# Score blocks of the agent-attention and squared-ReLU kernel: their TensorE passes get the scheduler's highest priority

## The chip, the cores and the metric

The kernel runs on one core of one Trainium2 chip. The metric is the device time of one execution in microseconds (us). All times of the profile's rows count from the start of its span.

## The reference

Per batch (4 batches, 12480 tokens of 128 channels, 49 agents), attention goes through the agents, and its output goes through a two-layer network with a squared ReLU:

```python
a2k = sm(agents, k)            # softmax over the 12480 keys, scale 1/sqrt(128)
agent_v = a2k @ v
q2a = sm(q, agents)            # softmax over the 49 agents
x = (q2a @ agent_v).reshape(49920, 128)
h = np.maximum(x @ w_in, 0.0)  # 2048 columns
out = h * h @ w_out
```

All data are float32.

## The kernel before

**The main chain.** The attention's last product and the first layer are folded: a table per batch (`aw_hi` and `aw_ex`, 98 agent rows in high and low parts by 2048 columns) lets the first layer read the query weights (`w` and `x`) directly. A query block has 960 tokens, in two halves of 480 (the constant `G`). For each half the loop over `k` goes through 2048 columns in 8 steps of two groups of 128 columns. The loop issues two steps at a time, which is called a *round* here: 416 rounds in all, 8 to a query block. In a round TensorE does 12 passes of the second layer for earlier steps (`second`, tile `o`, three passes for each of four column groups: high by high, high by low, low by high), then 4 passes `h<-w,aw_hi` and 4 short passes `h<-x,aw_ex` (`first`, two tiles `h` of two banks each, from a pool of three). ScalarE (ACT) then does for each `h` tile a ReLU (`r`) and a square (`g_hi`), VectorE (DVE) the product `r*h` (into `gg`, or back into `h`), and DVE or GpSimd (POOL) the low part `g_lo`. `queued` ties each of these instructions behind the one before it on its engine, so that the main chain's own order on each engine is fixed; all of them are recorded at line 59, because `queued` issues them.

**The work beside it.** Queries of later blocks (`queries`) and keys and values of the next batch (`background`) are generators. `step` takes a few of their steps per round; from then on a scheduler decides, by priority and by a simulated time line, where their instructions stand among those of the main chain, since they are only tied behind the prologue. By default priority follows the order in which the code was recorded. All that work shares one PSUM bank, the pool `ps_a` with the tile `psa`, in turns: score blocks of keys (`psa<-ag,kt`) or queries (`psa<-ag,qt`), transposes of the query weights (`psa<-identr,pp`, line 381, two groups of 4 per query block), value sums (`psa<-vs,e`, 8 passes, line 302) and table pieces.

**A score block.** `scores` and `queries` call `tiled` for each of 8 groups of 120 or 128 tokens, and `tiled` cuts a group into strips of 32 tokens (`CT`): each strip is loaded as the stationary operand and writes 32 partitions of `psa`. A block is 32 such passes of 49 columns; in the trace each float32 pass is two matmuls, so a block shows as x64. After the block DVE takes the maximum (`m`, line 362) and the difference (`e`, line 364) of a query block, ACT the exponential, DVE the sum and its inverse (`z`, lines 369 to 371), POOL the product and the low part of the weights, and PE the transposes, from which ACT copies `w` (line 386). Small DMAs on SyncE's queue then fill the rest of `w` and `x`. `w` and `x` have two buffers per half, so that a block's weights lie where those of the block two before lay.

The main chain's own short passes already stand in such a context (`first`):

```python
with tc.high_priority():
    for t, out in enumerate(outs):
        rows = slice(t * 32, t * 32 + NL)
        queued(nc.tensor.matmul, nc.tensor, out, state[b]["lo"][rows, c // 2, :], x[rows, :], start=False, stop=True)
```

Of the kernel before, what the change touches and what calls it, by code (L numbers as in the profile page):

```python
# [32 lines left out]
CT = 32  # L33
# [4 lines left out]
def agent_attention_relu2(ctx: ExitStack, tc: tile.TileContext, qT, kT, v, agT, w_in, w_out, outT):  # L38
# [36 lines left out]
    pe, act, dve, pool, sync = (Ordered(e) for e in (nc.tensor, nc.scalar, nc.vector, nc.gpsimd, nc.sync))  # L75
# [22 lines left out]
    for base in (NA, -NA):  # L98
        nc.gpsimd.affine_select(
            out=quad.rearrange("p h a -> p (h a)"), in_=quad.rearrange("p h a -> p (h a)"),  # L100
# [76 lines left out]

    def tiled(out, stationary, moving):
        n = stationary.shape[1]
        for at in range(0, n, CT):  # L180
            up = min(at + CT, n)
            pe.matmul(out[at:up, :], stationary[:, at:up], moving, start=True, stop=True)  # L182

    def scores(b, i, kt):
        st = state.setdefault(b, {"s": []})
        _, rows, nt = blocks[i]
        if alone[0]:
            h = ps_h.tile([P, 2, 512], F32, name="h")[:rows, :, :].rearrange("p h (t x) -> p h t x", x=P)
            n = nt // 2
            for t in range(nt):  # L190
                out = h[:, t // n, t % n, : 2 * NA]
                keys = kt[:, t * rows : (t + 1) * rows]
                pe.matmul(out, keys, ag[:, :2, :].rearrange("c b a -> c (b a)"), start=True, stop=True)
            sv = h[:, :, :n, :NA]
        else:
            sv = bank()[:rows, : nt * NA].rearrange("p (t a) -> p t a", a=NA)
            for t in range(nt):
                tiled(sv[:, t, :], kt[:, t * rows : (t + 1) * rows], ag[:, b, :])
        yield
        s = sp.tile([P, NT, NA], F32, name="s")  # L200
        st["s"].append(s)
        if i == 0:
            st["mx"] = small.tile([P, NT, NA], F32, name="mx")
        s, mx = (x[:rows, :nt, :] for x in (s, st["mx"]))
        if alone[0]:
            s, mx = (x.rearrange("p (h t) a -> p h t a", h=2) for x in (s, mx))
        if i == 0:
            dve.tensor_copy(mx, sv)
        else:
            dve.tensor_max(mx, mx, sv)  # L210
        act.copy(s, sv)  # L211
# [139 lines left out]
    def queries(g):  # L351
# [6 lines left out]
        for t in range(NT):  # L358
            tiled(sv[:, t, :], qt[:, t * TP : (t + 1) * TP], ag[:, b, :])
# [140 lines left out]
    with tc.tile_pool(name="pre", bufs=PRE) as pre, tc.tile_pool(name="dec", bufs=2) as dec:  # L500
# [39 lines left out]
        for i in range(NK):  # L540
# [9 lines left out]
            if i in between:  # L550
                n = between[i]
# [82 lines left out]
```

## Time and profile before

| | |
|---|---|
| median of 3 runs | 2038.29 us (2037.62 to 2038.71) |
| profiled execution | 2038.58 us, its span 2036.8 us, so 1.78 us lie around the span |
| granted TensorE clock over the span | 0.99 |
| TensorE (PE) busy | 1993.6 us, 98% of the span |
| ACT, DVE, POOL busy | 1776.5, 1663.8, 1271.1 us |

The first 105 us or so are a prologue (weights, keys and values of the first batch); the rest is the 416 rounds. PE, the matmul row, counts as busy from the start of a matmul to its modelled end, and neighbours overlap; how much time a piece of work takes from the others is therefore read from starts: how long after the first `o` pass of one round the first `o` pass of the next one begins.

### The profile page before, as it was taken

To read this page: it belongs to the slowest core of one execution; us is meant where nothing else is said; L and a number is where in the kernel's file an instruction comes from. 1 tells how busy PE (TensorE), PEld (TensorE's weight loads), DVE (VectorE), ACT (ScalarE), POOL (GpSimd) and SP (SyncE) were. 2 spreads that over 40 slices of the span, in tenths; PEclk is the share of its full clock that TensorE was granted. 3 is DMA by queue.
4 is the path that set the end of the run, shared out by engine and by line. 5 is a ranking of instruction groups with operands and counts; after the bars stand their busy time and mean duration, and the time that the engine had idled before them with its cause. 6 is when DMAs were issued, how large, how long until landed. Compare 5 with 4: busy or idle time off the path is not lost.

```text
span 2036.8 us, 40065 instructions
## 1 busy us (share of the span) xinstructions
PE 1993.6 (98%) x15188; PEld 1493.9 (73%) x15188; DVE 1663.8 (82%) x1843; ACT 1776.5 (87%) x2100; POOL 1271.1 (62%) x1103
## 2 busy tenths in 40 slices
PE   8599999999999999999999999999999999999999
PEld 8477777777777777777777777777777777777777
DVE  5678888888888888888888888888888888888887
ACT  2388999989888999999898899998998989889897
POOL 2555877766555687776565577776555656556565
PEclk8799999999999999999999999999999999999999
DMA  8243121121123221211113212211111111111100
GB/s 311 86 139 92 62 63 51 63 73 50 48 69 97 71 66 59 72 46 63 58 36 97 88 43 68 63 58 41 38 46 45 34 44 34 41 43 38 41 25 27
DMA packets 55976, 131.89 MB, mean 65 GB/s; under 512 B 6712, under 2 KB 35336, under 8 KB 55784
## 3 DMA queue, kind: packets, MB, share of 16 engines
q1 hardware_dynamic: 55784, 129.33, 19.8%
q8 instruction: 120, 1.97, 0.4%
q14 instruction: 72, 0.59, 0.1%
HBM read 80.97 MB, written 25.56 MB: 52 GB/s over the span
## 4 chain that ended last, share of the span: by engine, by line
PE 50%; DMA 1%; DVE 1%; ACT 1%; issue 0%; SPq 0%; ACTq 0%; DVEq 0%
PE o L59 31%; PE h L59 16%; PE psa L182 2%; PE psa L381 1%; DMA kt<-in_kT 0%; PE psa L302 0%; PE psa L335 0%; DMA x<-w 0%; ACT r L59 0%; DVE gg L59 0%; DVE h L59 0%; DVE g_lo L59 0%; ACT g_hi L59 0%; DVE ob L59 0%; SPq L391 0%
## 5 line engine op out<-in xcount | busy, mean ns | idle before, releaser
L432 POOL TENSOR_TENSOR g_lo<-gg,g_hi 128x480 fp32r<-128x480 f32 x832 | 999.5, 1223 | 684.1 <-DVE gg L59 534.9
L59 ACT ACTIVATE r<-h 128x960 f32<-128x960 f32 x832 | 801.2, 963 | 127.2 <-PE h L59 120.1
L59 ACT ACTIVATE g_hi<-r 128x960 fp32r<-128x960 f32 x832 | 837.7, 1007 | 32.7 <-issue 0.4
L59 DVE TENSOR_TENSOR h<-r,h 128x960 f32<-128x960 f32 x416 | 481.9, 1158 | 166.3 <-ACT r L59 165.8
L59 DVE TENSOR_TENSOR gg<-r,h 128x960 f32<-128x960 f32 x416 | 477.5, 1148 | 82.6 <-ACT r L59 76.1
L59 PE MATMUL o<-g_hi,wo_hi 128*128 128x480 f32 x1664 | 538.3, 404 | 0.0
L59 DVE TENSOR_TENSOR g_lo<-h,g_hi 128x960 fp32r<-128x960 f32 x416 | 480.4, 1155 | 36.6 <-ACT g_hi L59 7.9
L59 PE MATMUL h<-w,aw_hi 128*128 128x480 f32 x1664 | 493.6, 403 | 15.9 <-DVE gg L59 13.5
L59 PE MATMUL o<-g_lo,wo_hi 128*128 128x480 f32 x1664 | 495.0, 378 | 0.0
L59 PE MATMUL o<-g_hi,wo_lo 128*128 128x480 f32 x1664 | 494.5, 378 | 0.0
L59 PEld LDWEIGHTS o<-g_hi,wo_hi 128*128 128x128 f32 x1664 | 280.3, 188 | 118.4 <-issue 78.0
L59 PEld LDWEIGHTS o<-g_hi,wo_lo 128*128 128x128 f32 x1664 | 312.5, 188 | 47.4
L59 PEld LDWEIGHTS o<-g_lo,wo_hi 128*128 128x128 f32 x1664 | 312.8, 188 | 46.9
L59 PEld LDWEIGHTS h<-w,aw_hi 128*128 128x128 f32 x1664 | 283.5, 189 | 76.2 <-DVE gg L59 27.8
L59 PE MATMUL h<-x,aw_ex 19*128 19x480 f32 x1664 | 205.8, 480 | 1.0 <-DMA x<-w 0.9
L59 PEld LDWEIGHTS h<-x,aw_ex 19*128 19x128 f32 x1664 | 80.4, 181 | 142.1 <-issue 138.3
L59 DVE COPY ob<-o 128x480 f32<-128x480 f32 x104 | 68.3, 657 | 42.7 <-PE o L59 42.6
L237 POOL TENSOR_TENSOR vs<-vt,vs 128x1024 fp32r<-128x1024 f32 (+1 forms) x39 | 81.7, 2096 | 5.6 <-ACT vs L235 5.4
L182 PEld LDWEIGHTS psa<-ag,qt 128*32 128x32 f32 (+1 forms) x3200 | 47.4, 107 | 50.7 <-issue 44.8
L182 PE MATMUL psa<-ag,qt 128*32 128x49 f32 (+1 forms) x3200 | 68.2, 211 | 0.0
L381 PEld LDWEIGHTS psa<-identr,pp 120*98 120x98 f32 x408 | 51.1, 166 | 9.0 <-ACT s L211 0.7
L386 ACT CAST w<-psa 98x480 fp32r<-98x480 f32 x102 | 55.6, 545 | 1.7 <-PE psa L381 1.5
(113 smaller groups left out, 965.1 us busy)
## 6 DMA issues: line engine op xcount, KB each, us to landing
qt<-in_qT SPq DMA_DIRECT2D x52, 480.0 KB
out_T<-ob SPq DMA_DIRECT2D x104, 240.0 KB
kt<-in_kT SPq DMA_DIRECT2D x36, 512.0 KB
vt<-in_v SPq DMA_DIRECT2D x36, 512.0 KB
x<-w SPq DMA_DIRECT2D x416, 35.6 KB
ahead<-in_kT SPq DMA_DIRECT2D x12, 512.0 KB
ahead<-in_v SPq DMA_DIRECT2D x12, 512.0 KB
w<-w SPq DMA_DIRECT2D x104, 56.2 KB
```

Source lines behind the costliest of these rows:

```text
L59: ins = issue(*args, **kw)
L182: pe.matmul(out[at:up, :], stationary[:, at:up], moving, start=True, stop=True)
L237: eng.tensor_sub(out[:, :, n : n + w], x, out[:, :, :w].bitcast(F32))
L381: pe.matmul(pt[:K2, t * TP : (t + 1) * TP], pp[:, j * (NT // 2) + t, :], identr, start=True, stop=True)
L386: act.copy(w[:K2, :], pt[:K2, :G])
L432: nc.gpsimd.tensor_sub(lo[:, n, :], gg[:, n, :], hi[:, n, :].bitcast(F32))
```

## The change

`tiled` opens a context of highest priority around its loop, so that the scheduler takes the passes of one call as soon as they are ready, before any other ready instruction of TensorE. No instruction is added or removed, no size, tile or buffer is changed.

```diff
     def tiled(out, stationary, moving):
         n = stationary.shape[1]
-        for at in range(0, n, CT):
-            up = min(at + CT, n)
-            pe.matmul(out[at:up, :], stationary[:, at:up], moving, start=True, stop=True)
+        with tc.high_priority():
+            for at in range(0, n, CT):
+                up = min(at + CT, n)
+                pe.matmul(out[at:up, :], stationary[:, at:up], moving, start=True, stop=True)
```

What the scheduler makes of it can be read from the order in which the built programs issue their instructions. Before, 51 of the 86 blocks of 32 passes beside the main chain stand in one piece and 35 in several: 15 in five pieces (9, 4, 8, 4 and 7 passes), 3 in five (9, 8, 9, 3 and 3), and 17 in three (7, 6, 19 or near it). Together the 35 blocks have 106 pieces more than blocks. Now all 86 are in one piece. The three tail blocks of 6 passes were whole and are.

On PE, at a key block of the third batch that stood in three pieces before (tiles `w` and `x` are the query weights of the block in work):

```order
L59 MATMUL o<-g_lo,wo_hi 128x480 x2
L182 MATMUL psa<-ag,kt 32x49 x9
L59 MATMUL h<-w_6083,aw_hi 128x480 x2
L182 MATMUL psa<-ag,kt 32x49 x4
L59 MATMUL h<-w_6083,aw_hi 128x480 x2
L59 MATMUL h<-x_6084,aw_ex 128x480 x4
```

The third piece, of 19 passes, stands in the round behind. Now, on PE at a key block of the same stretch:

```order
L59 MATMUL o<-g_lo,wo_hi 128x480 x2
L183 MATMUL psa<-ag,kt 32x49 x32
L59 MATMUL h<-w_6032,aw_hi 128x480 x4
L59 MATMUL h<-x_6033,aw_ex 128x480 x4
L59 MATMUL o<-g_hi,wo_hi 128x480 x2
```

The block moved into one place, between the second layer's passes and the first layer's.

On PE, in the last batch, the query block of tile `psa_19791` before (its first two pieces; three more follow in the next two rounds):

```order
L59 MATMUL o_19693<-g_lo_19613,wo_hi_108 128x480 x2
L182 MATMUL psa_19791<-ag_82,qt_19751 32x49 x3
L182 MATMUL psa_19791<-ag_82,qt_19751 24x49
...
L59 MATMUL h_19713<-w1_19239,aw_hi_17165 128x480 x2
L182 MATMUL psa_19791<-ag_82,qt_19751 32x49 x2
...
L59 MATMUL h_19714<-w1_19239,aw_hi_17165 128x480 x2
L59 MATMUL h_19713<-x1_19240,aw_ex_17166 128x480 x2
```

And the same block now:

```order
L59 MATMUL o_19307<-g_lo_19281,wo_hi_108 128x480 x2
L183 MATMUL psa_19791<-ag_82,qt_19751 32x49 x3
L183 MATMUL psa_19791<-ag_82,qt_19751 24x49
...
L59 MATMUL h_19367<-w0_19188,aw_hi_17165 128x480 x2
L59 MATMUL h_19368<-w0_19188,aw_hi_17165 128x480 x2
L59 MATMUL h_19367<-x0_19189,aw_ex_17166 128x480 x2
```

It became whole, and it stands 7 rounds earlier among the passes of the main chain. From the second batch's values on, most of the work on `psa` moved up by 6 to 10 rounds with it, transposes and value sums too.

On ACT, the copy of the transposed query weights into `w0_19960` before (line 386; `r` and `g_hi` are the main chain's):

```order
L59 ACTIVATE r_19994<-h_19964 128x960
L59 ACTIVATE g_hi_19997<-r_19994 128x960
L386 CAST w0_19960<-psa_19955 98x480
L59 ACTIVATE r_20024<-h_20014 128x960
L59 ACTIVATE g_hi_20028<-r_20024 128x960
```

And now:

```order
L59 ACTIVATE r_19516<-h_19485 128x960
L59 ACTIVATE g_hi_19519<-r_19516 128x960
L387 CAST w0_19960<-psa_19955 98x480
L59 ACTIVATE r_19540<-h_19530 128x960
L59 ACTIVATE g_hi_19544<-r_19540 128x960
```

The copy kept its place behind a `g_hi`, but it moved 10 rounds up. There the round's last passes that read `w0_19188`, whose buffer `w0_19960` takes over, stand directly behind the transposes on PE, where before they lay rounds back.

## Rows read from the trace of the kernel before

**Rows 1.** The page: busy time by engine, share of the span, instructions.
```profile
PE 1993.6 (98%) x15188; PEld 1493.9 (73%) x15188; DVE 1663.8 (82%) x1843; ACT 1776.5 (87%) x2100; POOL 1271.1 (62%) x1103
```

**Rows 2.** Busy time by stretch: stretch, its length, then PE, PEld, DVE, ACT, POOL.
```profile
300.00:400.00 100.00, 99.58 (x631) 75.95 (x630) 83.90 (x90) 95.28 (x114) 74.90 (x63) 1.00 0.18 58
...
1503.00:1975.00 472.00, 472.00 (x3042) 344.66 (x3041) 391.38 (x411) 421.44 (x473) 273.53 (x236) 1.00 0.12 39
```

**Rows 3.** Waits, whole program: who waited for whom, us in total, times, longest.
```profile
ACT r L59 <- PE h L59: 120.1, 171, 1.2
...
PE h L59 <- DVE gg L59: 13.5, 15, 7.0
...
PEld h L59 <- DMA x<-w: 3.5, 8, 0.8
```

**Rows 4.** Timeline of PE, a round without other work: start, length, instruction.
```profile
1678.93 0.69 PE L59 MATMUL o<-g_hi,wo_hi 128*128 128x480 f32 x2
...
1683.00 0.70 PE L59 MATMUL o<-g_hi,wo_hi 128*128 128x480 f32 x2
```

**Rows 5.** Timeline of PE, two rounds that each hold a whole block.
```profile
604.73 0.70 PE L59 MATMUL o<-g_hi,wo_hi 128*128 128x480 f32 x2
...
609.85 0.70 PE L59 MATMUL o<-g_hi,wo_hi 128*128 128x480 f32 x2
...
634.99 0.70 PE L59 MATMUL o<-g_hi,wo_hi 128*128 128x480 f32 x2
...
637.77 0.89 PE L182 MATMUL psa<-ag,qt 128*32 128x49 f32 x64
...
640.07 0.70 PE L59 MATMUL o<-g_hi,wo_hi 128*128 128x480 f32 x2
```

**Rows 6.** Timeline of PE, three rounds that hold a block in five pieces.
```profile
1664.26 0.69 PE L59 MATMUL o<-g_hi,wo_hi 128*128 128x480 f32 x2
...
1667.06 0.45 PE L182 MATMUL psa<-ag,qt 128*32 128x49 f32 x18
...
1669.35 0.69 PE L59 MATMUL o<-g_hi,wo_hi 128*128 128x480 f32 x2
...
1677.15 0.37 PE L182 MATMUL psa<-ag,qt 128*32 128x49 f32 x14
```

**Rows 7.** Timeline of PE: first passes around a three-piece and another five-piece block.
```profile
399.23 0.71 PE L59 MATMUL o<-g_hi,wo_hi 128*128 128x480 f32 x2
...
409.14 0.71 PE L59 MATMUL o<-g_hi,wo_hi 128*128 128x480 f32 x2
...
1224.50 0.71 PE L59 MATMUL o<-g_hi,wo_hi 128*128 128x480 f32 x2
...
1239.25 0.70 PE L59 MATMUL o<-g_hi,wo_hi 128*128 128x480 f32 x2
```

**Rows 8.** Timeline of ACT in the second round of rows 6.
```profile
1669.45 0.97 ACT L59 ACTIVATE r<-h 128x960 f32<-128x960 f32 x1 [1.13 <-PE h L59]
```

**Rows 9.** Timeline of POOL, DVE and PE near 305 us, and line 370's group.
```profile
304.02 2.21 POOL L237 TENSOR_TENSOR vs<-vt,vs 128x1024 fp32r<-128x1024 f32 x1 [0.41 <-ACT vs L235]
...
305.00 1.27 DVE L370 TENSOR_SCALAR z<-z 120x8 f32<-120x8 f32 x1
...
307.38 0.70 PE L59 MATMUL h<-w,aw_hi 128*128 128x480 f32 x2 [0.42 <-DVE gg L59]
...
1650.08 0.16 DVE L370 TENSOR_SCALAR z<-z 120x8 f32<-120x8 f32 x1
...
L370 DVE TENSOR_SCALAR z<-z 120x8 f32<-120x8 f32 x51 | 21.7, 426 | 0.2
```

**Rows 10.** Timeline of PE and ACT at a group of transposes and the copy behind it.
```profile
1658.50 0.48 PE L381 MATMUL psa<-identr,pp 120*98 120x120 f32 x4
1658.81 0.65 PE L59 MATMUL h<-w,aw_hi 128*128 128x480 f32 x2
...
1659.31 0.54 ACT L386 CAST w<-psa 98x480 fp32r<-98x480 f32 x1
```

## The prediction

> **What bounds the kernel now.** I read the page's busy times first: PE is busy for 98% of the span, ACT for 87%, DVE for 82% [rows 1]. A busy PE proves little, since its matmuls overlap in the record, so I looked at two stretches. In the last batch, where only queries run beside the main chain, PE never pauses in 472 us, and ACT works for 421.44 of them, 89%; in the values' stretch PE is busy for 99.58 of 100 us and ACT for 95.28 [rows 2]. Then the waits: ACT waited 171 times for PE's `h`, 120.1 us in all, while PE waited only 13.5 us for DVE's `gg`, of which 7.0 us are one wait [rows 3]. So PE sets the pace of the rounds nearly everywhere, and a microsecond that leaves PE's sequence leaves the time, as long as ACT and DVE can follow. The third view is the timeline of PE, where rounds can be compared from first pass to first pass.
>
> **The change part by part.** A round without other work takes 1683.00 − 1678.93 = 4.07 us [rows 4]. A round with a whole block takes 640.07 − 634.99 = 5.08 us, and another 609.85 − 604.73 = 5.12 us [rows 5]; I take their mean, 5.10, so a whole block costs 1.03 us.
>
> A block in five pieces runs through three rounds, from 1664.26 [rows 6] to 1678.93 [rows 4]: 14.67 us, less three plain rounds (12.21), is 2.46 us. The other kind of five pieces takes 1239.25 − 1224.50 = 14.75 us [rows 7], so 2.54 us. A block in three pieces takes two rounds, 409.14 − 399.23 = 9.91 us [rows 7], less 8.14, so 1.77 us. All have the same 32 passes as a whole block. What they have more is the number of times that PE goes from the main chain's passes of 128 columns to strips of 32 columns and back.
>
> In one piece each saves the difference to 1.03 us: 1.43, 1.51 and 0.74 us. The order of the programs gives the counts: 15, 3 and 17. The sum is 15 × 1.43 + 3 × 1.51 + 17 × 0.74 = 21.45 + 4.53 + 12.58 = 38.6 us. As a check, that is 106 pieces fewer at 0.36 us each, and the three kinds alone give 0.36 (1.43 over four pieces), 0.38 (1.51 over four) and 0.37 (0.74 over two), so the price goes with the number of pieces, whatever their lengths. The 51 blocks that were whole, and the three tails, save nothing.
>
> Does PE's gain reach the end? In the last batch's 13 blocks (18.6 us of the sum) yes by these rows: ACT itself stands for 1.13 us waiting for PE in a round with pieces [rows 8], and ACT's 421.44 us in a stretch that shrinks from 472 to about 453 are 93%. For the other 22 blocks (20.0 us) the room is smaller, because of the 95.28 of 100 us; that is the first rival below.
>
> The moves cost nothing that I can find, but each has a bound. A whole block in front of the four `w` passes gives ACT its next `h` later by up to 1.03 us in one round instead of by less in three; the rounds of rows 5 show it at no cost beyond 1.03. The copy of `w` on ACT, 50 times, now waits for the two `w` passes behind the transposes, the last readers of the buffer that it overwrites. In the row the transposes end at 1658.98, the copy starts at 1659.31, and the two passes end at 1659.46 [rows 10], so the copy would be later by some 0.15 us here and by 0.48 us (1659.46 − 1658.98) if ACT were free at once. I take nothing, since ACT has 0.2 to 0.45 us to spare in a round by its busy shares (5 and 11% of 4.07); the bounds are 50 × 0 and 50 × 0.15 = 7.5 us. SyncE's queue issues the small copies into `x` behind it, and behind those the next query load, outputs and the next batch's keys or values; these are asked for later by the same 0.15 to 0.48 us, but all of the query work stands rounds earlier, so the weights have more time to land than before. That removes at most the 3.5 us in which PE waited for `x` [rows 3].
>
> The inverse of the sums (`z`, DVE, line 370) is the one step that shows how a shift may cost. Its work is tiny, 0.16 us, but beside a value conversion of 2.21 us on POOL it took 1.27 us, the product behind it was late, and PE stood 0.42 us; over all 51 it took 426 ns on the mean [rows 9]. It will still come about two rounds behind its score block, and the value sums move up with it, so that I let it cost what it costs now: a change of 0. [...] The sum by rows alone stays at 38.6 us.
>
> The profiled execution took 2038.58 us (span 2036.8 and 1.78 around it), 0.3 us over the median, which is no difference here. 2038.58 − 38.6 = 2000.0 us. I hold what a measurement can tell from no change to be 0.2%, 4 us.
>
> **The rivals.**
> 1. *ACT or DVE sets the pace where values run.* In the stretch of 300 to 400 us the three split blocks would take 2.2 us out of PE's 99.58, and ACT's 95.28 of 97.8 would be 97%: near enough to full that PE may wait for `h` to come free. For it speaks that these PE waits are already in the trace (0.42 us in rows 9); against it, that all of PE's waits for DVE's `gg` are only 13.5 us now [rows 3]. Half to all of the 20.0 us of the 22 blocks would be lost: 2010 to 2020 us.
> 2. *`z` meets POOL each time* (the other side). The shift brings each query's `z` beside a POOL instruction: 1.27 − 0.16 = 1.11 us on DVE per query block, and if PE follows in full, 50 × 1.11 = 55.5 us, so 2000.0 + 55.5 = 2055.5 us. It decides from 38.6 / 50 = 0.77 us per query block on; the PE wait seen, 0.42 us, is below that. Against it: the last batch has no value conversions, and the mean of 426 ns says that some of it is already paid.
> 3. *The waits go as well.* With query work rounds ahead, PE's waits for `gg` other than the longest (13.5 − 7.0 = 6.5 us) and for `x` (3.5 us) vanish too: 2000.0 − 10.0 = 1990 us. For it speaks only the earlier place.
> 4. *Nothing.* If the pieces only filled time in which PE would have waited anyway, whole blocks leave the same time as waits: 2038 us. Against it: whole blocks in rows 5 cost 1.03 us with no wait beside them, and ACT waited for PE in the pieces' rounds.
>
> **How the numbers follow.** The sum: 0.73, with its own range of 1993 to 2008 (10 us less by rival 3's waits in part, 7.5 us more by the copies). Rival 1: 0.15, of which about half lies below 2013. Rival 2: 0.04. Rival 3 in full: 0.05. Rival 4: 0.03. The prediction is 2000 us. A range of 1990 to 2013 holds the sum, rival 3 and half of rival 1, about 0.85. Faster by over 0.2% are the sum and rivals 1 and 3: 0.93; within 0.2% rival 4: 0.03; slower rival 2: 0.04.
>
> **What would show it.** In the timeline of PE of the changed kernel every block of 32 passes stands as x64, and a round that holds one takes about 5.1 us; the last batch's 8 rounds of a query block last 1.4 us less than before. PE is still busy for 98% or more, over a span of about 1998 us; ACT's and DVE's busy times are what they were, within a few microseconds, and their shares rise by 2%. Rival 1 would show in PE waits for DVE's `gg` that grow by 10 us or more in the values' stretches; rival 2 as a mean of line 370 over 1 us; rival 3 as waits below 8 us. The prediction is wrong if a whole block costs more than 1.03 us in its new place, by a wait for the bank `psa` or for `qt` to land, which PE, serving in order, would pass on to all passes behind it.

## The result and the profile after

The changed kernel takes 2008.97 us (median of 4 runs, 2008.32 to 2009.03) against 2038.16 us for the kernel before in the same comparison: a ratio of 0.9856, with a 95% interval of 0.9839 to 0.9873. It is 29.2 us faster. The prediction was 2000.0 us with a range of 1990 to 2013 us: the direction and the cause held, and 9 us of the gain did not come.

The page's busy times after, as in [rows 1]:

```profile
PE 1960.0 (98%) x15188; PEld 1492.7 (74%) x15188; DVE 1690.4 (84%) x1843; ACT 1777.6 (89%) x2100; POOL 1272.3 (63%) x1103
```

ACT and POOL do what they did, within 2 us. PE's busy time fell by 33.6 us. DVE's rose by 26.6 us, although no instruction was added (23.4 of it in the addition of the query sums, below): that is the first sign of what went wrong. The stretches that answer to [rows 2] (stretch, length, then PE, PEld, DVE, ACT, POOL):

```profile
300.00:400.00 100.00, 99.36 (x691) 76.10 (x690) 84.48 (x93) 95.12 (x114) 76.67 (x64) 1.00 0.20 65
1474.00:1940.00 466.00, 461.34 (x3066) 347.79 (x3066) 411.77 (x411) 428.29 (x480) 278.23 (x239) 1.00 0.12 39
```

In the last batch PE, which never paused before, now stands for 4.7 of 466 us. The values' stretch looks as before. The timeline of PE in the last batch shows where (start, length, instruction; the first `o` passes of four rounds, and the block):

```profile
1579.00 0.69 PE L59 MATMUL o<-g_hi,wo_hi 128*128 128x480 f32 x2
...
1581.80 0.90 PE L183 MATMUL psa<-ag,qt 128*32 128x49 f32 x64
...
1584.11 0.70 PE L59 MATMUL o<-g_hi,wo_hi 128*128 128x480 f32 x2
...
1588.19 0.70 PE L59 MATMUL o<-g_hi,wo_hi 128*128 128x480 f32 x2
...
1592.94 0.70 PE L59 MATMUL o<-g_hi,wo_hi 128*128 128x480 f32 x2
```

The whole block's round takes 5.11 us, as in [rows 5], and the next one 4.08 us, as in [rows 4]. The one after that takes 4.75 us and holds no other work: 0.67 us are lost there. The timeline of the same rounds on DVE, POOL and PE says why:

```profile
1586.39 0.55 DVE L370 TENSOR_REDUCE z<-e 120x8 f32<-120x392 f32 x1
...
1586.94 2.40 POOL L433 TENSOR_TENSOR g_lo<-gg,g_hi 128x480 fp32r<-128x480 f32 x2 [2.46 <-DVE z L370]
1586.97 1.21 DVE L371 TENSOR_SCALAR z<-z 120x8 f32<-120x8 f32 x1
...
1588.22 0.20 DVE L372 RECIPROCAL z<-z 120x8 f32<-120x8 f32 x1
1588.34 1.14 DVE L59 TENSOR_TENSOR h<-r,h 128x960 f32<-128x960 f32 x1
...
1590.69 1.15 DVE L59 TENSOR_TENSOR gg<-r,h 128x960 f32<-128x960 f32 x1
...
1591.89 0.48 PE L59 MATMUL h<-w,aw_hi 128*128 128x480 f32 x1 [0.35 <-DVE gg L59]
```

Eight numbers per partition get 1e-9 added, and it takes 1.21 us: it ends as the first half of POOL's `g_lo`, begun 0.03 us earlier, ends (two halves in 2.40 us). Everything behind it on DVE is late, the product `gg` ends at 1591.84, and PE, which needs the `h` tile that `gg` frees, starts its second pair of `w` passes at 1591.89. Over the program (the group of this line, with its mean in ns, and the wait of PE for `gg` in us, times, longest):

```profile
L371 DVE TENSOR_SCALAR z<-z 120x8 f32<-120x8 f32 x51 | 45.1, 884 | 1.0
```
```profile
PE h L59 <- DVE gg L59: 21.7, 30, 7.4
```

The mean was 426 ns before [rows 9] and the wait 13.5 us [rows 3].

### The profile page after: what moved, and what is told of

Its sections match the earlier page's. It is cut to its first block, busy times and chain, and to the rows that moved or that the text cites. A ratio compares the mean times of both kernels' runs of the same rounds, so it can differ in the third digit from the quotient of the medians.

```text
span 2007.2 us, 40193 instructions
## 1 busy us (share of the span) xinstructions
PE 1960.0 (98%) x15188; PEld 1492.7 (74%) x15188; DVE 1690.4 (84%) x1843; ACT 1777.6 (89%) x2100; POOL 1272.3 (63%) x1103
## 5 line engine op out<-in xcount | busy, mean ns | idle before, releaser
L433 POOL TENSOR_TENSOR g_lo<-gg,g_hi 128x480 fp32r<-128x480 f32 x832 | 1000.6, 1224 | 645.7 <-DVE gg L59 437.0
L59 DVE TENSOR_TENSOR g_lo<-h,g_hi 128x960 fp32r<-128x960 f32 x416 | 480.5, 1155 | 37.7 <-ACT g_hi L59 4.3
L59 PE MATMUL h<-w,aw_hi 128*128 128x480 f32 x1664 | 476.4, 397 | 23.6 <-DVE gg L59 21.7
L59 PEld LDWEIGHTS h<-w,aw_hi 128*128 128x128 f32 x1664 | 290.5, 189 | 87.2 <-DVE gg L59 39.1
L238 POOL TENSOR_TENSOR pp<-e,pp 120x392 fp32r<-120x392 f32 x51 | 49.2, 966 | 3.3 <-ACT pp L236 3.3
L183 PEld LDWEIGHTS psa<-ag,qt 128*32 128x32 f32 (+1 forms) x3200 | 37.9, 108 | 16.7 <-issue 10.3
```

The source lines that it names most:

```text
L59: ins = issue(*args, **kw)
L238: eng.tensor_sub(out[:, :, n : n + w], x, out[:, :, :w].bitcast(F32))
L433: nc.gpsimd.tensor_sub(lo[:, n, :], gg[:, n, :], hi[:, n, :].bitcast(F32))
```

## The experiments

Theory A: the missing 9 us are the addition in `z`, held up beside POOL's `g_lo` and passed on to PE. Theory B: a whole block delays `h`, and ACT and DVE fall behind whatever `z` takes. Eight kernels were run, each against the kernel before, whose median was 2037.62 us beside e1 to e4 and 2037.53 us beside e5 to e8. With the 2038.16 us beside the changed kernel, times of different comparisons carry some 0.6 us against each other.

**e1_no_add.** The changed kernel without the addition.

```diff
         dve.reduce_sum(z, e, axis=AX.X)
-        dve.tensor_scalar_add(z, z, 1e-9)
         dve.reciprocal(z, z)
```

> The changed kernel without line 371, the addition of 1e-9 to the query sums (left out; the sums are at least 1, since each block's maximum is subtracted). Theory A (the 9 us that the change fell short are DVE waits at that addition, which POOL's g_lo holds up for 1.2 us in 34 or so of 50 query blocks): the waits of PE for DVE's gg behind a score block vanish, also those that the kernel before already had; 20 us of lateness over the rounds' medians sit there, so 1989 to 1996 us. Theory B (a whole block makes h late, and ACT and DVE fall behind whatever z takes): only 45 us of DVE time off PE's path goes, at most 2 us less: 2007 to 2009 us.

Measured: 1990.89 us, 0.9773 of the kernel before (0.9759 to 0.9788). Theory A; theory B is out, since leaving out a step that takes 0.16 us when free gave 18.1 us. The same place of the last batch, on DVE and POOL:

```profile
1574.14 0.56 DVE L370 TENSOR_REDUCE z<-e 120x8 f32<-120x392 f32 x1
...
1574.73 0.20 DVE L371 RECIPROCAL z<-z 120x8 f32<-120x8 f32 x1
...
1575.52 1.16 DVE L59 TENSOR_TENSOR h<-r,h 128x960 f32<-128x960 f32 x1 [0.58 <-ACT r L59]
...
1574.70 2.41 POOL L432 TENSOR_TENSOR g_lo<-gg,g_hi 128x480 fp32r<-128x480 f32 x2 [2.80 <-DVE z L370]
```

POOL starts `g_lo` as the sum ends, just as in the changed kernel, and the reciprocal runs beside it in 0.20 us, not held. DVE then even waits for ACT. On PE the rounds behind the block:

```profile
1571.87 0.70 PE L59 MATMUL o<-g_hi,wo_hi 128*128 128x480 f32 x2
...
1575.95 0.70 PE L59 MATMUL o<-g_hi,wo_hi 128*128 128x480 f32 x2
...
1580.14 0.69 PE L59 MATMUL o<-g_hi,wo_hi 128*128 128x480 f32 x2
```

4.08 and 4.19 us, where the changed kernel has 4.08 and 4.75: the held addition costs 0.56 us here. In the last batch PE and ACT run the same instructions in the same order in both kernels (2818 and 459 of them from the 313th product `gg` on), so that the addition alone makes this difference; in the batches before it the order differs in places. PE's waits for `gg` are 10.2 us, of which 7.2 us are one wait in the prologue's end:

```profile
PE h L59 <- DVE gg L59: 10.2, 6, 7.2
```

**e2_before_no_add.** The same line taken out of the kernel before; the blocks are in pieces again.

```diff
-        dve.tensor_scalar_add(z, z, 1e-9)
```

> The kernel before without the same addition (left out). Its order has 131 pieces more than blocks where the kernel before has 106. If each piece costs 0.36 us whatever stands beside it, it lies 131 x 0.36 = 47 us above the changed kernel without the addition: under theory A 2036 to 2043 us, about the kernel before. If pieces only fill time in which PE would wait anyway, it lies within 10 us of the changed kernel without the addition.

Measured: 2035.37 us, 0.9989 (0.9979 to 0.9999). It is 44.5 us above e1, for 131 pieces: 0.34 us each, with no addition in either kernel. This is the price of a piece without the addition, and it agrees with the 0.36 us from rounds of one kernel, although e1 and e2 also differ in where the blocks stand. Pieces do not fill time in which PE would wait here. (The expected 2036 to 2043 was 0.6 us too high at its lower end.)

**e3_two_adds.** The suspected step doubled.

```diff
         dve.tensor_scalar_add(z, z, 1e-9)
+        dve.tensor_scalar_add(z, z, 0.0)
```

> The changed kernel with a second addition (of zero) behind line 371 in each query block. Theory A: the second one meets the second half of POOL's g_lo as the first met the first, 1.2 us more on DVE in some 34 blocks, of which PE pays at least half: 2025 to 2050 us. Theory B: 50 x 0.07 us of DVE time beside the path: 2009 to 2012 us.

Measured: 2055.96 us, 1.0096 (1.0075 to 1.0116): slower than the kernel before, 47.0 us above the changed kernel, and 6 us more than theory A's upper end. Both additions are held; in the last batch the first ends with the first half of `g_lo` and the second with the second (1.22 us from 1576.33 and 1.15 us from 1577.58, beside POOL's 2.40 us from 1576.30). Their means:

```profile
L371 DVE TENSOR_SCALAR z<-z 120x8 f32<-120x8 f32 x51 | 44.9, 880 | 1.0
L372 DVE TENSOR_SCALAR z<-z 120x8 f32<-120x8 f32 x51 | 40.0, 784 | 1.0
```

Why it overshot stands in the last section.

**e4_queries_only.** Highest priority for the query blocks alone.

```diff
-    def tiled(out, stationary, moving):
+    def tiled(out, stationary, moving, first=False):
...
-        with tc.high_priority():
+        with tc.high_priority() if first else ExitStack():
...
-            tiled(sv[:, t, :], qt[:, t * TP : (t + 1) * TP], ag[:, b, :])
+            tiled(sv[:, t, :], qt[:, t * TP : (t + 1) * TP], ag[:, b, :], first=True)
```

> Highest priority for the passes of query blocks alone. All 50 query blocks are whole, but 8 key blocks now stand in 5 or 6 pieces, 34 pieces more than in the changed kernel. By 0.36 us a piece 2009.0 + 12.4 = 2021 us, if the waits at z stay those of the changed kernel (2016 to 2026). If a piece costs less where keys run, below 2014 us.

Measured: 2017.57 us, 0.9905 (0.989 to 0.9919), 8.6 us above the changed kernel for 34 pieces. That is 0.25 us a piece taken alone. The waits at `z` did not stay: the mean of line 371 is 707 ns here, and PE's wait for `gg` 17.4 us, 4.3 us less than in the changed kernel; if that wait counts in full, the pieces cost 12.9 us, 0.38 each (an estimate). The query blocks carry the gain.

**e5_quarter_g_lo and e6_one_g_lo.** POOL's `g_lo` in four instructions for each tile, and in one, in place of two.

```diff
-            for n in range(2):
-                nc.gpsimd.tensor_sub(lo[:, n, :], gg[:, n, :], hi[:, n, :].bitcast(F32))
+            for n in range(4):
+                y = slice(n % 2 * (G // 2), (n % 2 + 1) * (G // 2))
+                nc.gpsimd.tensor_sub(lo[:, n // 2, y], gg[:, n // 2, y], hi[:, n // 2, y].bitcast(F32))
```
```diff
+            nc.gpsimd.tensor_sub(lo, gg, hi.bitcast(F32))
```

> The changed kernel with POOL's g_lo in four instructions of 240 columns for each tile in place of two of 480. If the addition z is held until the POOL instruction beside it ends, its mean over 51 (884 ns in the changed kernel, 160 ns when free) falls to about half of the excess, 450 to 600 ns, and with it half of PE's lateness at z: 1997 to 2004 us. If z is late for another reason (it waits for a semaphore, or for DVE's own work), the mean stays near 884 ns and the time at 2009 us or, by POOL's two more starts for each tile, above.

> The changed kernel with POOL's g_lo in one instruction of 960 columns for each tile in place of two of 480. If z is held for the length of the POOL instruction, its mean rises to 1500 to 1700 ns (2.4 us where it meets one), and PE pays most of 1.2 us more in some 30 blocks: 2030 to 2050 us. If not, 884 ns and 2009 us.

Measured: 1999.59 us with four, 0.9815 (0.9799 to 0.9831), and 2047.45 us with one, 1.0051 (1.0036 to 1.0066). The groups of `g_lo` and of the addition, with four:

```profile
L434 POOL TENSOR_TENSOR g_lo<-gg,g_hi 128x240 fp32r<-128x240 f32 x1664 | 1120.8, 707 | 525.3 <-DVE gg L59 378.6 <-ACT r L59 50.0 <-DVE z L370 40.0
...
L371 DVE TENSOR_SCALAR z<-z 120x8 f32<-120x8 f32 x51 | 33.0, 647 | 1.0
```

and with one:

```profile
L432 POOL TENSOR_TENSOR g_lo<-gg,g_hi 128x960 fp32r<-128x960 f32 x416 | 942.0, 2264 | 722.2 <-DVE gg L59 484.0 <-ACT r L59 69.4 <-ACT g_hi L59 58.5
...
L371 DVE TENSOR_SCALAR z<-z 120x8 f32<-120x8 f32 x51 | 71.0, 1391 | 1.0
```

POOL instructions of 0.71, 1.22 and 2.26 us give additions of 647, 884 and 1391 ns on the mean, and 1999.6, 2009.0 and 2047.5 us. The means mix held additions with free ones; single held ones of the last batch show the lengths. With four (POOL's `g_lo`, the addition beside it, and the addition two query blocks later):

```profile
1582.72 2.69 POOL L434 TENSOR_TENSOR g_lo<-gg,g_hi 128x240 fp32r<-128x240 f32 x4 [2.18 <-DVE z L370]
1582.75 0.70 DVE L371 TENSOR_SCALAR z<-z 120x8 f32<-120x8 f32 x1
...
1651.87 0.70 DVE L371 TENSOR_SCALAR z<-z 120x8 f32<-120x8 f32 x1
```

and with one:

```profile
1644.88 2.27 POOL L432 TENSOR_TENSOR g_lo<-gg,g_hi 128x960 fp32r<-128x960 f32 x1 [2.93 <-PE o L59]
1644.91 2.26 DVE L371 TENSOR_SCALAR z<-z 120x8 f32<-120x8 f32 x1
...
1717.13 2.27 DVE L371 TENSOR_SCALAR z<-z 120x8 f32<-120x8 f32 x1
```

In these, as at 1586.97 us of the changed kernel, the addition lasts until the POOL instruction beside it ends, at each of the three lengths: 0.70, 1.21 and 2.26 us. The steps shown at 1586.97 us (changed kernel), 1574.73 us (e1, the reciprocal) and 1650.08 us (kernel before, [rows 9]) return two query blocks later at:

```profile
1657.12 1.21 DVE L371 TENSOR_SCALAR z<-z 120x8 f32<-120x8 f32 x1
```
```profile
1643.74 0.20 DVE L371 RECIPROCAL z<-z 120x8 f32<-120x8 f32 x1
```
```profile
1722.00 0.17 DVE L370 TENSOR_SCALAR z<-z 120x8 f32<-120x8 f32 x1
```

Half of each distance is the time of a query block's eight rounds in the last batch:

| kernel | addition | eight rounds |
|---|---|---|
| before (five pieces, addition free) | 0.16 us | 35.96 us |
| e1 (whole, no addition) | none | 34.51 us |
| e5 (whole, four `g_lo`) | 0.70 us | 34.56 us |
| changed (whole, two `g_lo`) | 1.21 us | 35.08 us |
| e6 (whole, one `g_lo`) | 2.26 us | 36.11 us |

From 0.70 to 1.21 us the addition grows by 0.51 and the rounds by 0.52; from 1.21 to 2.26 us by 1.05 and 1.03. So the first 0.65 us or so are free (in e1 DVE stood 0.58 us for ACT just behind this place), and PE pays the rest in full. Of e6's whole time some 10 us go with a lower TensorE clock, 0.985 against 0.99 (an estimate, last section). With four the mean is a little above the expected 450 to 600 ns, with one below the expected 1500 to 1700; the times lie where they were expected. Over the whole program four win 9.4 us although `g_lo` takes POOL 120 us longer (1120.8 us against 1000.6): POOL's busy time is not the bound; what counts is how long the addition lasts beside POOL, 647 ns on the mean against 884.

**e7_two_tensor_add.** The number in the addition replaced by a tile in SBUF, which POOL fills once in the prologue.

```diff
-        dve.tensor_scalar_add(z, z, 1e-9)
+        dve.tensor_add(z, z, eps)
```

> The changed kernel with line 371 as an addition of two tensors in SBUF (z and a constant tile of 1e-9) in place of a tensor and a number. If an addition with two SBUF inputs is held beside POOL like the one with a number, 2006 to 2012 us and a mean over 700 ns; if only the form with a number is held, about 200 ns and the time without the addition, 1989 to 1995 us.

Measured: 2009.51 us, 0.9863 (0.9849 to 0.9878), the changed kernel's time, and the same mean:

```profile
L373 DVE TENSOR_TENSOR z<-z,eps 120x8 f32<-120x8 f32 x51 | 45.0, 882 | 1.0
```

The addition with two inputs in SBUF is held like the one with a number, 882 ns on the mean against 884.

**e8_keys_only.** Highest priority for the key blocks alone (the edit of e4, with `first=True` in `scores`).

> Highest priority for the passes of key blocks alone. Two key blocks become whole (four pieces fewer by themselves), but the order has 106 pieces more than blocks, as the kernel before, and the query blocks stand where they stood. By 0.36 us a piece no change: 2035 to 2039 us. If the key blocks' place alone shifts the background work, a few us either way.

Measured: 2041.02 us, 1.0018 (1.0009 to 1.0027), 3.5 us slower than the kernel before and 2 us beyond what was expected. The query blocks are in their old pieces, so that the keys give no gain. The mean of line 371 is 570 ns, against 426 before; whether that is all of the 3.5 us was not tried.

## Why the prediction was right in its cause and 9 us off

- **The pieces.** Right. All 86 blocks are whole, a block's round takes 5.11 us, and e2 against e1 gives 0.34 us a piece where the rounds of the kernel before gave 0.36. For 106 pieces that is 36.0 us against the predicted 38.6. In the last batch, where a block stood in five pieces, the eight rounds of a query block lose 35.96 − 34.51 = 1.45 us by e1, where 1.43 were predicted.
- **The addition in `z`.** This is the term that was mis-sized: "I let it cost what it costs now: a change of 0". It costs 18.1 us in the changed kernel (2008.97 − 1990.89). What it cost before can be estimated: e2 less its 25 pieces more (25 × 0.34 = 8.5) is 2026.9 us, against 2037.62 for the kernel before beside it, so 10.7 us. The rise is then 7.4 us. That 36.0 − 7.4 = 28.6 us comes near the 29.2 measured is no check, since the 7.4 are worked out from the same medians. The last batch is a check: the addition was free there and is held now in all 13 blocks, at 35.08 − 34.51 = 0.57 us each, which is 7.4 us. There a query block's rounds gain 35.96 − 35.08 = 0.88 us, not the 1.4 that the prediction named as a sign.
- **Where the step failed.** The prediction saw one addition held beside a value conversion and took that as the partner. The partner that counts is `g_lo`, a step of the main chain in every round. (`queued` does not tie this one: its rows stand at line 432 or 433, not 59.) Of the 51 additions, 25 now last 0.94 us or more beside a `g_lo`, where 2 did before; beside value conversions of `vs` it is 7, where it was 8. Those two stand in the trace of before, 1.22 us at 156.53 and 1.21 at 197.3, and the prediction did not look at them. Whether the two meet is decided by where the addition stands in DVE's sequence. Before, in the last batch, a `g_lo` and a `gg` of DVE stood between the sum and the addition, and it ran free (0.16 us at 1650.08 in [rows 9]), over before POOL began:

```profile
1647.48 0.55 DVE L369 TENSOR_REDUCE z<-e 120x8 f32<-120x392 f32 x1
1647.96 1.15 DVE L59 TENSOR_TENSOR g_lo<-h,g_hi 128x960 fp32r<-128x960 f32 x1
1649.02 1.14 DVE L59 TENSOR_TENSOR gg<-r,h 128x960 f32<-128x960 f32 x1
...
1650.33 2.40 POOL L432 TENSOR_TENSOR g_lo<-gg,g_hi 128x480 fp32r<-128x480 f32 x2 [2.11 <-DVE z L370]
```

- **Where it stands now.** The addition stands directly behind the sum, as POOL's `g_lo` begins, and it took about 1.2 us in each of the last batch's 13 blocks. "The last batch has no value conversions" was counted against rival 2, and the last batch is where it came in full.
- **The rivals.** Rival 2 had the mechanism, at a seventh of its price: before had paid part of it already, and PE pays about 0.57 us of the 1.05 us by which a held addition grows. In the last batch the addition lasted until the POOL instruction beside it ended, at 0.70 us in e5, 1.21 us in the changed kernel and 2.26 us in e6; with two inputs in SBUF (e7) its mean was the same, 882 ns. The reciprocal, at 0.20 us beside `g_lo` in e1, was not held. Why the one is held and the other not is not shown. Rival 1 did not come as it was put: in e1, with all blocks whole too, PE's waits for `gg` fall to 3.0 us beside the one of 7.2. Rival 3's waits grew instead of going, from 13.5 to 21.7 us; they go once the addition does.
- **The moves.** Right at nothing: the copy of `w` on ACT waited for PE for 0.2 us in all. The sign given for rival 2, a mean of line 370 (now 371) over 1 us, was set too high; 884 ns and DVE's 26.6 us more were the sign.
- **The range.** 2008.97 us lies 1 us outside the sum's own range of 1993 to 2008. That it lies within 1990 to 2013 is in part luck: the room above 2008 was made for rival 1, and the loss that filled it came by rival 2's mechanism, which had 0.04.

e1 is the best kernel of the study, 46.7 us faster than the kernel before it was measured with.

## What to carry to other kernels

Where TensorE is the bound, count how often it goes between passes of different shapes, not only the passes: 32 strips in five pieces took 2.46 us and in one 1.03. When an edit lets a scheduler move work, look on the other engines at what now stands beside the moved instructions; here an instruction of 0.16 us took 1.2 us by its place, and TensorE paid what went beyond the 0.65 us or so that its engine had to spare. An addition that rounding swallows (1e-9 to sums of at least 1) is best left out: 18.1 us here. Where it has to stay, shorter GpSimd instructions beside it are worth a try: `g_lo` in four in place of two won 9.4 us here.

## What was not expected of the hardware

**In e3 short waits on PE were followed by a lower clock, not every time.** In e3 PE stood twice in one round of the last batch, and the passes behind it were slow. The timeline of PE:

```profile
1581.36 0.70 PE L59 MATMUL h<-w,aw_hi 128*128 128x480 f32 x2 [0.99 <-DVE g_lo L59]
1582.42 0.70 PE L59 MATMUL h<-w,aw_hi 128*128 128x480 f32 x2 [0.36 <-DVE gg L59]
...
1584.44 1.00 PE L59 MATMUL o<-g_hi,wo_lo 128*128 128x480 f32 x2
1585.24 1.00 PE L59 MATMUL o<-g_lo,wo_hi 128*128 128x480 f32 x2
...
1586.84 0.60 PE L59 MATMUL o<-g_hi,wo_lo 128*128 128x480 f32 x2
1587.28 0.59 PE L59 MATMUL o<-g_lo,wo_hi 128*128 128x480 f32 x2
```

and the stretches around it, with the granted clock behind the five busy times:

```profile
1577.50:1583.50 6.00, 4.65 (x25) 2.98 (x21) 5.80 (x8) 4.82 (x6) 3.01 (x4) 0.99 0.03 11
1583.50:1589.50 6.00, 6.00 (x29) 4.68 (x25) 5.05 (x5) 4.19 (x5) 4.75 (x5) 0.72 0.11 41
1589.50:1596.00 6.50, 6.50 (x38) 5.27 (x35) 4.36 (x4) 5.89 (x8) 2.39 (x2) 1.00 0.09 24
```

After waits of 0.99 and 0.36 us the granted clock was 0.72 over 6 us, with pairs of passes 0.80 us apart for part of that stretch, and then 1.00 again, with 0.44 us. By the starts of the sums, the eight rounds from 1575.73 us, which hold this stretch, took 37.82 us, and the next eight, from 1613.55, took 36.22: 1.6 us lost. Four of the last batch's 12 distances in e3 are such long ones (37.8 to 38.1 us), and four in e6 (37.7 us against 36.1; granted clock 0.66 from 1796 to 1801 us). The waits alone do not decide it: in e3 PE stood 0.99 us at 1655.41 and 0.97 us at 1691.67 for the same `g_lo` of DVE, and the clock stayed at 1.00 from 1650 to 1660 and from 1690 to 1700 us. What decides it is not shown.

Over the span the clock of the profiled e3 is 0.985 and the changed kernel's 0.99. By that difference some 0.005 × 2050.8 = 10 us were lost (an estimate, from two rounded shares; it counts the missing share of the clock as lost time, which for the stretch above gives 0.28 × 6 = 1.7 us, where 1.6 us were lost). e6 has 0.985 too. The four runs of e3 go with the clock: 2052.86 and 2052.89 us at 0.985, 2059.04 at 0.982, 2061.74 at 0.979; those of e6 likewise, from 2045.62 us at 0.985 to 2050.91 at 0.981. Such a loss is more than the 6 us by which e3 overshot; that it is the reason is an inference. In the changed kernel, where PE's one wait at that place is 0.35 us, the last batch's clock is 1.00. e3 and e6 are also the two kernels in which PE waits often for DVE's `g_lo` (16.2 and 13.8 us, 18 times each).
